# Four moves in the written order of steps of a fused mLSTM cell and GELU layer

## The chip, the cores and the metric

The kernel runs on one core of a Trainium2 chip. The metric is device time in microseconds (us). Engines work side by side, each through its own queue in the order in which the program gives instructions: PE (matrix multiplies), DVE (vector), ACT (activation functions), POOL (GpSimd) and SP, which here issues most DMA transfers. An engine whose next instruction waits does nothing else in the meantime.

## The reference, cut to what matters

First an mLSTM cell over `q, k, v, o_gate` of shape (4, 8, 768, 40) and gates `i_gate, f_gate` of shape (4, 8, 768), then a two-layer feed-forward block with exact GELU:

```python
for t in range(S):
    m_new = maximum(f[t] + m, i[t])
    f_stab, i_stab = exp(f[t] + m - m_new), exp(i[t] - m_new);  m = m_new
    C = f_stab * C + i_stab * outer(v[t], k[t])
    n = f_stab * n + i_stab * k[t]
    y[t] = sigmoid(o[t]) * (C @ q[t]) / maximum(abs(n @ q[t]), 1)
x = y.transpose(0, 2, 1, 3).reshape(3072, 320)
out = gelu_exact(x @ w_in) @ w_out        # w_in 320 x 2048, w_out 2048 x 320
```

## The kernel before

The sequence of 768 is cut into six chunks of 128, numbered 0 to 5. Within a chunk the recurrence is written as attention with decays, and only a state of each head goes from chunk to chunk. The four batch entries of a chunk are called turns 0 to 3 here; each has eight heads. Each chunk's 512 rows of y then go through the feed-forward block. From chunk 1 on, its matrix products are made of three products of split operands (a high part, a low part and a sum, named `hi`, `lo` and `mid` or `all`).

The work of two chunks is interleaved: while the feed-forward block of chunk c runs, the cell of chunk c+1 is computed, and the cell of chunk c+2 is begun. Nothing schedules this but strings written by hand. Each word of a string is a step, a letter with an index, and `play` calls the steps from left to right; an engine's queue is what falls to it in that order. `FRONT` holds chunk 0 and all preparation, `SECOND` the feed-forward block of chunk 1 with the cell of chunk 2, `LATER` those of chunks 2, 3 and 4, and `LAST` that of chunk 5. An index of 4 or more on a cell letter means the cell after next: `M4` is turn 0 of it.

The steps that the change touches, or that stand next to it:

- `U0` to `U3` (`up`, L1055 and L1061 on PE): the four parts of x @ w_in into PSUM tiles `pu`, two at a time from the same banks as other steps of the cell.
- `g0` to `g15` (`gelu`): block n of 128 hidden features. ACT does GELU (L1068, `g_whole`) and the high part (L1069), then DVE the low part (L1070) and the rest (L1071). The first GELU after other functions has an ACT table load in front of it.
- `d0` to `d15` (`down`, L1075 on PE): block n times `w_out`, three products for each of four turns.
- `y0` to `y15` (`out_mid`, L1030 on DVE): the sum part of the weights for `d` of that index, in one of four places `w_out_mid`, which are used in turn.
- `i5` to `i14` (`load_in`, L1004 on SP): the reload of a stored sum part of `w_in` (256 KB each) into one of five places. `i10` and `i11` bring the parts that the next chunk's `U0` reads.
- `M` (`mask`, L469 on POOL) and `W` (`weights`, L495 on ACT): the masking and the exponentials of a turn's decay matrix, tile `W`, which `B` (`load_M`, L211 on SP) brings as two 512 KB loads.
- `K` and `Q` in `LATER`, `(` and `)` in `FRONT` (`turn_k`, `turn_q`, L511 on DVE): the transposing of a turn's k and q from `blocks` into `kT` and `qT`. `L` and `[` (`load_blocks`, L189 on SP) load `blocks` from the copies `kq_d`, which `+` (L180 on SP) makes in DRAM.
- `C`, `h` (PE L620, L631): the state read and its update. `D` (L538 on POOL): values times decays, tile `vw`.
- `S` (`scores_two`) multiplies scores into `W` (L573 on DVE); `V` (`values`, PE L657 and DVE L662).
- `Y` (`finish`, L671 to L674 and L679 on DVE): five steps for a turn's gated and normalised y, in tile `ob`.
- `t` (`twice`, L686, on ACT from chunk 2 on): a small copy of a turn's last 64 columns of y, twice, into `y_rest`.
- `X` (`turn_y`, PE L695, ACT L705): the transposing of a turn's y from `ob` and `y_rest` into `px`, and the high part of x. `R` (`split_x`, DVE L716 and L717): its other parts.
- `J` and `O` (`load`, L171 and L173 on SP): k, v and gate loads. `F` in `FRONT` (L959 on PE): chunk 0 times `w_out`, one row block at a time; `a` and `b` (ACT L1015, DVE L1022) prepare parts of `w_out`.

The word `t0` means `twice(0)`: it needs the result of `Y0`, and `X0` needs it. `y_rest` is one tile for all turns, so `t1` also waits until PE has read what `t0` wrote.

Of the kernel before, what the change touches and what calls it, by code (L numbers as in the profile page):

```python
# [28 lines left out]
    g1 c1 J y1 s2 K x0 t3 x1 v2 g2 O4 J B4 g3 c2 y2 s3 B5 K x2 K L5 J T0 K v3 A y3 M1 x3 c3 G0 M0 H O7 O6 O5 J  # L29
    J i5 u0 L6 u1 K W0 J W1 I4 A K S0 T1 C0 J j5 i6 V0 i7 u2 G2 K U M2 L7 S1 J G1 K U i8 j6 W2 J j7 i9 C1 T2 K  # L30
    M3 f2 S2 V1 Y0 T3 J Y1 C2 e j8 W3 j9 K K K J S3 J C3 f3 K X0 B8 J K R0 B9 h5 J h6 h7 K J V2 K Y2 J J Z Z K
    K V3 X1 J K r F J h8 h9 F a0 a1 F K b0 b1 F a2 a3 F b2 b3 F F F J K X2 G3 F F J K J Y3 F J K R1 a4 a5 b4 b5 a6 b6 K B10 p + + + + F X3 a7 b7 F J J Z Z R2 R3
    a8 F (0 )0 [1 Z a9 a10 <0 <1 >0 >1 a11 a12 a13 a14 a15 z0 z1 b8 b9 b10 b11 b12 b13 b14 b15 B11 F F """
CELL = "MWGVYXRKQDCSht"
LATER = """
    U0 E0 E1 E2 E3 K1 Q1 L2 D0 D1 y0 y1 y2 y3 C0 h0 M2 M3 g0 g1 g2 g3 i5 i6 +
    U1 i7 i8 i9 g4 d0 g5 y4 d1 g6 y5 d2 g7 y6 S0 d3 K2 Q2 L3 y7 W2 W3 G0 G1 G2 G3 +
    U2 i10 i11 g8 d4 g9 V0 V1 K3 Q3 B4 B5 J0 J1 d5 g10 d6 g11 S2 L4 d7 y8 y9 y10 y11
    U3 + M4 M5 Y0 Y1 D2 D3 K4 W4 W5 t0 i12 i13 i14 g12 d8 g13 y12 d9 g14 X0 t1 R0 y13 d10 g15 X1 R1 C2 h2 O0 O1 d11 V2 Y2 t2 y14 B6 J2 d12 V3 Y3 Q4 L5 y15 B7 d13 X2 t3 R2 d14 X3 R3 d15 + O2 O3"""

SECOND = """
    z2 U0 z3 z4 K1 Q1 L2 D0 D1 y0 y1 y2 y3 C0 h0 M2 M3 g0 g1 g2 g3 i5 i6 + +
    U1 i7 i8 i9 g4 d0 g5 y4 d1 g6 y5 d2 g7 y6 S0 d3 K2 Q2 L3 y7 W2 W3 G0 G1 G2 G3 +
    U2 i10 i11 + g8 d4 g9 V0 V1 K3 Q3 B4 B5 J0 J1 d5 g10 d6 g11 S2 L4 d7 y8 y9 y10 y11
    U3 + M4 M5 Y0 Y1 D2 D3 K4 W4 W5 t0 i12 i13 i14 g12 d8 g13 y12 d9 g14 X0 t1 R0 y13 d10 g15 X1 R1 C2 h2 O0 O1 d11 V2 Y2 t2 y14 B6 J2 d12 V3 Y3 Q4 L5 y15 B7 d13 X2 t3 R2 d14 X3 R3 d15 + O2 O3"""

LAST = """
    U0 E0 E1 E2 E3 y0 y1 y2 y3 g0 g1 g2 g3 U1 i5 i6 i7 i8 i9 x y12 y13 y14 y15 g4 d0 g5 y4 d1 g6 y5 d2 g7 y6 d3 y7
# [1141 lines left out]
```

## Time and profile before

| what | value |
|---|---|
| time, median of 3 runs | 452.74 us (451.29 to 452.99) |
| the profiled execution, time | 450.36 us |
| its span, first to last instruction | 448.6 us |
| PE busy | 435.4 us (97%) |
| DVE busy | 352.7 us (79%) |
| ACT busy | 283.9 us (63%) |
| POOL busy | 54.3 us (12%) |
| granted TensorE clock | 0.999 |
| U0 of chunks 1 to 5 starts at | 121.2, 192.0, 259.4, 327.1, 391.1 us |

All times of instructions below are counted from the start of the span. In a timeline row stand start, duration, engine, line, operation, tiles written and read, shapes and count, and in brackets the idle time of the engine ahead of it with what released it. In a row of the page's groups stand busy time and mean duration, and behind the bar the idle time ahead of the group's instructions and its releaser. `SPq` is SP's queue issuing DMA transfers.

### The profile page before, as it was taken

The numbers are of one execution on the slowest core, as the hardware profiler recorded it, in microseconds if no ns is written. First come the engines' busy times: TensorE is split into PE (matmuls) and PEld (weight loads), VectorE is DVE, ScalarE is ACT, GpSimd is POOL, SyncE is SP. The second block draws the span as 40 slices with busy tenths as digits, with TensorE's granted clock in tenths as the row PEclk, the third lists the DMA queues.
The fourth block names the chain that finished last, engine by engine and source line by source line (L and its number), as shares of the span: only waits on it lengthen the run. The fifth ranks groups of instructions, "written<-read, shape, count | busy, mean of one in ns | idle before, by whom it ended". The sixth has DMA issues, their size and how long they took to land.

```text
span 448.6 us, 13147 instructions
## 1 busy us (share of the span) xinstructions
PE 435.4 (97%) x5320; PEld 375.5 (84%) x5320; DVE 352.7 (79%) x759; ACT 283.9 (63%) x603; POOL 54.3 (12%) x82
## 2 busy tenths in 40 slices
PE   8999999999999998999999999999999999999996
PEld 7778788777778897888898888898888898989986
DVE  8797788877989599959599959599969598847540
ACT  4989999858958939137968037958137925244441
POOL 3001123030030022221021211021110000000000
PEclk9999999999999999999999999999999999999999
DMA  7998995898297478466687365696466412032001
GB/s 154 212 212 219 206 237 150 208 286 216 95 241 189 101 205 165 92 135 144 138 217 148 90 135 136 143 212 124 94 143 170 79 31 72 1 108 70 1 1 58
DMA packets 165785, 63.24 MB, mean 141 GB/s; under 512 B 148413, under 2 KB 151773, under 8 KB 165469
## 3 DMA queue, kind: packets, MB, share of 16 engines
q1 hardware_dynamic: 165004, 60.76, 58.2%
q0 software_dynamic: 400, 1.31, 0.7%
q8 instruction: 42, 0.69, 0.7%
q10 hardware_dynamic: 320, 0.33, 0.2%
q14 instruction: 19, 0.15, 0.1%
HBM read 55.63 MB, written 11.99 MB: 151 GB/s over the span
## 4 chain that ended last, share of the span: by engine, by line
PE 62%; DVE 12%; issue 10%; DMA 8%; ACT 5%; POOL 2%; SPq 1%; POOLq 0%; DVEq 0%; ACTq 0%
PE po L1075 21%; PE pu L1055 20%; PE pu L1061 6%; DMA W<-M_d 5%; PE po L959 4%; DMA kq_d<-in_q_dram 3%; PE pu L789 2%; ACT W L495 2%; DVE w_out_mid L1030 2%; DVE g_parts L1071 2%; PE ps L567 2%; PE ph L657 2%; DVE g_parts L1070 1%; PE pf L620 1%; PE px L695 1%
## 5 line engine op out<-in xcount | busy, mean ns | idle before, releaser
L1070 DVE SCALAR_TENSOR_TENSOR g_parts<-g_whole,g_parts 128x512 fp32r<-128x512 f32 x80 | 56.7, 709 | 43.4 <-ACT g_parts L1069 43.1
L1068 ACT ACTIVATE g_whole<-pu 128x512 f32<-128x512 f32 x80 | 47.4, 593 | 60.3 <-PE pu L1061 40.2
L1075 PE MATMUL po<-w_out_mid,g_parts 128*128 128x320 f32 x320 | 58.5, 299 | 0.0
L1069 ACT ACTIVATE g_parts<-g_whole 128x512 fp32r<-128x512 f32 x80 | 50.5, 631 | 8.8 <-PE po L1075 6.6
L1071 DVE TENSOR_TENSOR g_parts<-g_whole,g_parts 128x512 fp32r<-128x512 f32 x80 | 55.3, 691 | 0.0
L1055 PE MATMUL pu<-x_hi,w_in_hi 128*128 128x512 f32 x160 | 48.4, 384 | 0.2 <-DVE W L573 0.2
L1075 PE MATMUL po<-w_out_hi,g_parts 128*128 128x320 f32 x240 | 48.5, 316 | 0.0
L1075 PEld LDWEIGHTS po<-w_out_mid,g_parts 128*128 128x128 f32 x320 | 48.4, 189 | 0.0
L1055 PE MATMUL pu<-x_all,w_in_mid 128*128 128x512 f32 x160 | 47.6, 379 | 0.0
L1075 PE MATMUL po<-w_out_lo,g_parts 128*128 128x320 f32 x240 | 44.6, 299 | 0.0
L469 POOL TENSOR_SCALAR_AFFINE_SELECT W<-W 128x1024 f32<-128x1024 f32 (+2 forms) x20 | 22.2, 1111 | 153.2 <-DMA W<-M_d 144.6
L1075 PEld LDWEIGHTS po<-w_out_hi,g_parts 128*128 128x128 f32 x240 | 35.6, 190 | 4.4 <-issue 3.3
L495 ACT ACTIVATE W<-W,aT 128x128 f32<-128x128 f32 x128 | 38.8, 388 | 0.4 <-POOL W L469 0.3
L1075 PEld LDWEIGHTS po<-w_out_lo,g_parts 128*128 128x128 f32 x240 | 36.5, 189 | 0.2 <-issue 0.2
L959 PE MATMUL po<-w_out,g 128*128 128x320 f32 x128 | 35.0, 432 | 0.0
L1030 DVE TENSOR_TENSOR w_out_mid<-w_out_hi,w_out_lo 128x320 fp32r<-128x320 f32 x60 | 34.0, 588 | 0.1
L1055 PEld LDWEIGHTS pu<-x_all,w_in_mid 128*128 128x128 f32 x160 | 30.2, 189 | 4.3
L1055 PEld LDWEIGHTS pu<-x_hi,w_in_hi 128*128 128x128 f32 x160 | 29.1, 189 | 4.3 <-PE po L1075 0.4
L686 ACT COPY y_rest<-ob 128x128 f32<-128x128 f32 x16 | 4.7, 294 | 43.9 <-DVE ob L679 43.9
L959 PEld LDWEIGHTS po<-w_out,g 128*128 128x128 f32 x128 | 24.1, 190 | 9.7
L1075 PE MATMUL po<-w_out_part,g_parts 128*128 128x320 f32 x160 | 25.9, 305 | 0.0
L1075 PEld LDWEIGHTS po<-w_out_part,g_parts 128*128 128x128 f32 x160 | 22.5, 189 | 1.9 <-issue 1.7
(195 smaller groups left out, 835.9 us busy)
## 6 DMA issues: line engine op xcount, KB each, us to landing
w_in_mid<-w_in_mid_d SPq DMA_DIRECT2D x36, 256.0 KB, 6.6
W<-M_d SPq DMA_DIRECT2D x16, 512.0 KB, 6.6
bits<-in_moe_w_in_dram SPq DMA_DIRECT2D x20, 256.0 KB, 4.4
bits<-in_moe_w_out_dram SPq DMA_DIRECT2D x16, 320.0 KB, 4.9
blocks<-kq_d SPq DMA_DIRECT2D x32, 128.0 KB, 3.3
ob<-in_o_gate_dram SPq DMA_DIRECT2D x24, 160.0 KB, 5.9
out_dram<-o_sb SPq DMA_DIRECT2D x36, 80.0 KB, 2.0
g_parts<-w_in_mid_d SPq DMA_DIRECT2D x9, 256.0 KB, 5.8
```

What stands on the lines that cost most here:

```text
L469: nc.gpsimd.affine_select(out=x, in_=x, compare_op=OP.is_ge, fill=1.0e30, base=base, pattern=[[0, H], [1, x.shape[2]]], channel_multiplier=-1)
L495: nc.scalar.activation(out=W[n][:, h, :], in_=src, func=AF.Exp, scale=-1.0, bias=aT[:, self.c, r:r + 1])
L567: nc.tensor.matmul(ps[i][hip][halves[x ^ i], p, t], kT[i][r, p, halves[x]], qT[i][r, p, t], start=True, stop=True)
L959: nc.tensor.matmul(po[b], g.t[:, f, b * L:(b + 1) * L], w_row(n), start=(n == 0), stop=(n == NF - 1))
L1030: nc.vector.tensor_tensor(out=to, in0=hi, in1=lo, op=OP.add)
L1055: nc.tensor.matmul(in_pairs(pus[i][e]), w3(at[k])[n][:, e, i * P:(i + 1) * P], in_turns(x3[n][:, k, :]), start=(n == 0 and k == 0), stop=F ...
L1061: nc.tensor.matmul(in_pairs(pus[i][e]), w3(r)[n][h, q % 2, i * P:(i + 1) * P], in_turns(x3[n][h, NX, :]), start=False, stop=(n == 2), skip ...
L1068: nc.scalar.activation(out=whole, in_=self.pus[n // 4][n % 4 // 2][n % 2], func=AF.Gelu, scale=4097.0)
L1069: nc.scalar.activation(out=hi, in_=whole, func=AF.Copy, scale=PART)
L1070: nc.vector.scalar_tensor_tensor(out=lo, in0=whole, scalar=-1.0 / BASE, in1=hi, op0=OP.mult, op1=OP.add)
L1071: nc.vector.tensor_tensor(out=rest, in0=whole, in1=hi, op=OP.subtract)
L1075: nc.tensor.matmul(in_pairs(self.po[t]), x[:, t * L:(t + 1) * L], in_turns(w), start=(n == 0 and k == 0), stop=(n == NF - 1 and k == 2), s ...
```

## The change

No instruction is added or removed; four kinds of step move in the strings.

1. `(0 )0`, which transpose turn 0 of the third chunk's cell (chunk 2), move in `FRONT` from behind `a8 F` to ahead of the first `F`, behind `h9`. On DVE they come ahead of the first L1022 and of everything that stood between.
2. `y8 y9 y10 y11` stood at the end of the `U2` row. Now `Y0` comes first, then `y8 y9`, `Y1`, `y10 y11`.
3. `t0` stood ahead of `i12 i13 i14 g12`; now it stands behind `g12`.
4. `i10 i11` stood directly behind `U2`; now they stand directly ahead of `i12`. On SP they are passed by a copy into `kq_d` (`SECOND` alone), the two loads of `W`, the loads of k and v, a load of `blocks` and another copy into `kq_d`.

Moves 2 to 4 are in `SECOND` and in `LATER`, so they happen in chunks 1, 2, 3 and 4.

```diff
 FRONT = """
...
-    K V3 X1 J K r F J h8 h9 F a0 a1 F K b0 b1 F a2 a3 F b2 b3 F F F J K X2 G3 F F J K J Y3 F J K R1 a4 a5 b4 b5 a6 b6 K B10 p + + + + F X3 a7 b7 F J J Z Z R2 R3
-    a8 F (0 )0 [1 Z a9 a10 <0 <1 >0 >1 a11 a12 a13 a14 a15 z0 z1 b8 b9 b10 b11 b12 b13 b14 b15 B11 F F """
+    K V3 X1 J K r F J h8 h9 (0 )0 F a0 a1 F K b0 b1 F a2 a3 F b2 b3 F F F J K X2 G3 F F J K J Y3 F J K R1 a4 a5 b4 b5 a6 b6 K B10 p + + + + F X3 a7 b7 F J J Z Z R2 R3
+    a8 F [1 Z a9 a10 <0 <1 >0 >1 a11 a12 a13 a14 a15 z0 z1 b8 b9 b10 b11 b12 b13 b14 b15 B11 F F """
...
 LATER = """
...
-    U2 i10 i11 g8 d4 g9 V0 V1 K3 Q3 B4 B5 J0 J1 d5 g10 d6 g11 S2 L4 d7 y8 y9 y10 y11
-    U3 + M4 M5 Y0 Y1 D2 D3 K4 W4 W5 t0 i12 i13 i14 g12 d8 g13 y12 d9 g14 X0 t1 R0 y13 d10 g15 X1 R1 C2 h2 O0 O1 d11 V2 Y2 t2 y14 B6 J2 d12 V3 Y3 Q4 L5 y15 B7 d13 X2 t3 R2 d14 X3 R3 d15 + O2 O3"""
+    U2 g8 d4 g9 V0 V1 K3 Q3 B4 B5 J0 J1 d5 g10 d6 g11 S2 L4 d7
+    U3 + M4 M5 Y0 y8 y9 Y1 y10 y11 D2 D3 K4 W4 W5 i10 i11 i12 i13 i14 g12 t0 d8 g13 y12 d9 g14 X0 t1 R0 y13 d10 g15 X1 R1 C2 h2 O0 O1 d11 V2 Y2 t2 y14 B6 J2 d12 V3 Y3 Q4 L5 y15 B7 d13 X2 t3 R2 d14 X3 R3 d15 + O2 O3"""
...
 SECOND = """
...
-    U2 i10 i11 + g8 d4 g9 V0 V1 K3 Q3 B4 B5 J0 J1 d5 g10 d6 g11 S2 L4 d7 y8 y9 y10 y11
-    U3 + M4 M5 Y0 Y1 D2 D3 K4 W4 W5 t0 i12 i13 i14 g12 d8 g13 y12 d9 g14 X0 t1 R0 y13 d10 g15 X1 R1 C2 h2 O0 O1 d11 V2 Y2 t2 y14 B6 J2 d12 V3 Y3 Q4 L5 y15 B7 d13 X2 t3 R2 d14 X3 R3 d15 + O2 O3"""
+    U2 + g8 d4 g9 V0 V1 K3 Q3 B4 B5 J0 J1 d5 g10 d6 g11 S2 L4 d7
+    U3 + M4 M5 Y0 y8 y9 Y1 y10 y11 D2 D3 K4 W4 W5 i10 i11 i12 i13 i14 g12 t0 d8 g13 y12 d9 g14 X0 t1 R0 y13 d10 g15 X1 R1 C2 h2 O0 O1 d11 V2 Y2 t2 y14 B6 J2 d12 V3 Y3 Q4 L5 y15 B7 d13 X2 t3 R2 d14 X3 R3 d15 + O2 O3"""
```

## The prediction

> **What bounds the kernel now.** I read the page first, then PE's waits and timeline, then the timeline of all engines around each wait. By the page PE is busy nearly throughout, so only a stop of PE can be won back. The copy y_rest, which the change moves, sits behind 43.9 us of ACT idle time.
>
> ```profile
> PE 435.4 (97%) x5320; PEld 375.5 (84%) x5320; DVE 352.7 (79%) x759; ACT 283.9 (63%) x603; POOL 54.3 (12%) x82
> ...
> L686 ACT COPY y_rest<-ob 128x128 f32<-128x128 f32 x16 | 4.7, 294 | 43.9 <-DVE ob L679 43.9
> ```
>
> ACT is busy 63% of the span, so those 43.9 us are not a sum to claim. From 131 us on, PE's timeline shows real stops almost only at the transposes px (L695) near the end of a chunk, between the fourth up step (U3) and the next U0. Brackets give idle time and releaser.
>
> ```profile
> 177.85 0.33 PE L695 MATMUL px<-ident,y_rest 128*128 128x128 f32 x1 [1.45 <-ACT y_rest L686]
> ...
> 187.51 0.41 PE L695 MATMUL px<-ident,ob 128*128 128x128 f32 x2 [0.32 <-DVE ob L679]
> ...
> 254.91 0.41 PE L695 MATMUL px<-ident,ob 128*128 128x128 f32 x2 [0.31 <-DVE ob L679]
> ...
> 312.93 0.33 PE L695 MATMUL px<-ident,y_rest 128*128 128x128 f32 x1 [0.64 <-ACT y_rest L686]
> ...
> 324.96 0.41 PE L695 MATMUL px<-ident,ob 128*128 128x128 f32 x2 [0.72 <-DVE ob L679]
> ...
> 386.67 0.71 PE L1075 MATMUL po<-w_out_mid,g_parts 128*128 128x320 f32 x4
> 387.21 0.38 PE L695 MATMUL px<-ident,ob 128*128 128x128 f32 x2
> ```
>
> The last two rows, chunk 4, are undisturbed: px starts 0.54 after the group before it, and y_rest 0.22 after ob. Against those spacings chunk 1 loses 0.35+1.62+0.49+0.35 = 2.8 us, chunk 2 0.25+0.48+0.35 = 1.1, chunk 3 0.80+0.88 = 1.7, chunk 4 nothing: 5.6 us, the ceiling for the U3 edits. What leads to these stops, in chunk 2:
>
> ```profile
> 222.13 0.85 SPq L1004 DMA_DIRECT2D w_in_mid<-w_in_mid_d  x2
> ...
> 225.21 0.96 SPq L211 DMA_DIRECT2D W<-M_d  x2
> ...
> 231.73 1.28 ACT L495 ACT_TABLE_LOAD   x1 [2.83 <-DMA W<-M_d]
> ...
> 233.48 1.95 POOL L469 TENSOR_SCALAR_AFFINE_SELECT W<-W 64x1024 f32<-64x1024 f32 x2 [0.59 <-DMA W<-M_d]
> ...
> 234.27 3.38 DVE L1030 TENSOR_TENSOR w_out_mid<-w_out_hi,w_out_lo 128x320 fp32r<-128x320 f32 x4
> 235.51 1.79 POOL L538 TENSOR_TENSOR vw<-vb,ewT 128x328 f32<-128x328 f32 x2
> ...
> 238.61 0.49 DVE L679 TENSOR_TENSOR ob<-ob,den 128x320 f32<-128x320 f32 x1
> ...
> 239.14 0.30 ACT L686 COPY y_rest<-ob 128x128 f32<-128x128 f32 x1 [1.23 <-DVE ob L679]
> ...
> 239.46 1.28 ACT L1068 ACT_TABLE_LOAD   x1
> ...
> 240.47 0.70 DVE L511 STREAM_TRANSPOSE kT<-blocks 128x512 f32<-128x512 f32 x1
> ...
> 242.04 0.69 DVE L1070 SCALAR_TENSOR_TENSOR g_parts<-g_whole,g_parts 128x512 fp32r<-128x512 f32 x1 [0.87 <-ACT g_parts L1069]
> ```
>
> The loads W release the masks and exps; DVE does four sums, then Y0, which frees ACT's copy, gelu and split; DVE waits 0.87 for that split. From 242.04 to the last ob at 257.14 DVE has no idle row: an earlier L1070 passes on one for one to the px that stop PE. Chunks 1 and 3 read the same.
>
> **The front's two turns.** (0 and )0 are two L511 of 0.70 and 0.67 us. They leave 119.20 on DVE for a place after 101.2, where DVE idles 1.70 us for ACT before the L1022 at 102.87; their blocks were asked for at 76.08 and such a load lands in 4.2 us, so they do not wait. If that cover were gone they would cost 1.3 us of DVE, not of PE. The freed 1.3 us at 119 brings w_in_lo and the first w_in_mid earlier for U0, whose first pair at 121.17 shows 0.24 more than its spacing: at most 0.24. PE's 1.01 stop at 129.87 stays: it waits for the next turn, whose block loads SP issued at 121.84 and 124.78 because of the copies into kq_d, which do not move. Taken as 0.
>
> **Gelu ahead of the copy (t0).** The copy's 1.23 us wait (chunks 2 and 3; none in chunk 1) and its 0.30 leave the path to block 12. The exps end at 171.85, 237.91, 305.59; table 1.28, gelu 0.60, split 0.63 and gaps make ACT ready for L1070 at 174.4, 240.5, 308.2, instead of 174.64, 242.04, 309.72. Next late is DVE itself, whose kT turn ends at 173.81, 241.17, 309.21. The copy now delays block 13 by 0.30; DVE needs 1.2 us a block, so that hides. X0 reads y_rest later still (242.8 in chunk 2). In chunk 4 the gelu waits 1.18 us for PE's own products: nothing to win.
>
> **Y0 ahead of the sums.** PE's and POOL's orders do not change; on DVE the same instructions come in another order: Y0, two sums, Y1, two sums. The sums write w_out_mid places whose readers (d4 to d7) end before U3; d8 reads y8's first at 240.64, d10 y10's at 244.23: two us of slack or more. But POOL's masks and products run beside this stretch, and DVE pays:
>
> ```profile
> 368.31 1.70 DVE L1030 TENSOR_TENSOR w_out_mid<-w_out_hi,w_out_lo 128x320 fp32r<-128x320 f32 x4
> ...
> 169.45 0.70 DVE L672 TENSOR_SCALAR den<-far 128x8 f32<-128x8 f32 x1
> ```
>
> Four sums take 1.70 without POOL (chunk 4), 3.38 beside it; Y0's small L672 takes 0.70 beside it, 0.16 without. So each step, large or small, gets about one POOL instruction (0.8 to 1.2 us). Filling those slots with Y0's five short steps instead of sums of 0.43 does less work in them: in chunk 2 POOL's ends (234.56, 235.43, 236.36, 237.30) put Y0's end at 237.8, and 0.85+1.53+0.85+0.71 more ends kT at 241.74, 0.57 later than now. Alone this leaves L1070 earlier by 0.3 in chunks 2 and 3 (309.44 there) and 0.2 in chunk 1: 0.8 us in all. Without the port effect the sum would be 0.2+0.87+0.51 = 1.6. The Trainium skill, SBUF — State Buffer, Summary: rules for kernel authors, has a DVE operation with two SBUF inputs block fully until a GpSimd operation that reads SBUF ends. The sums agree with it, and it speaks against this edit. By its letter L672 and L674, with one input, would pass: kT in chunk 2 at about 241.3, and 1.4 us in all; the 0.70 row says otherwise.
>
> **Reloads i10, i11 moved on.** On SP they pass the W loads (B4, B5), the k and v loads, the blocks load (L4) and copies into kq_d, and now stand ahead of i12. Their issue takes 0.85 us; SP waits for PE's ph before W anyway, so issue wins nothing. Their 0.5 MB does: issued 3.1 us before W, on the same SP queue. DMA moved 171 GB/s in 223 to 226 and 285 GB/s in 226 to 229, other copies among it. If all had been gone by 225.21, W lands no sooner (0); if none, 0.52 MB / 285 GB/s = 1.8 us sooner. By 225.21 perhaps half had moved: I take 0.9. Both masks and exps follow W, so ACT is ready 0.9 sooner and POOL's slots begin beside L573, which they do not lengthen (1.78 against 1.76 in chunk 4). Redone with 0.9: kT ends near 173.9, 241.1, 308.8 (blocks, 0.27 late in chunk 3, come earlier too), so L1070 gains about 0.8, 0.9, 0.9. The reloads' own reader, U0, comes 17 us or more after the new place; a load takes 6.6. What they now share DMA with, gate loads and copies, is read a stage later; if that cover went, U0 would stand for the lateness.
>
> **Sum.** 0 + 0.8 + 0.9 + 0.9 + 0 = 2.6 us, within each chunk's stops. The profiled execution took 450.36 (span 448.6 and 1.8 around it), 0.5% below the median 452.74 of three runs (451.29 to 452.99): 447.8 on its scale, 450.1 on the median's. A measurement can tell 0.5%, 2.26 us, from no change.
>
> **Rivals.** *Small gain*: W lands no sooner and Y0 fills POOL's slots: 0.8 us, 451.9. For it: 3 us of head start for the reloads; against it: the 285 GB/s right after, DMA saturated. *All stops go*: W comes 1.8 sooner and PE bounds the tails: 4 to 5.5 us, about 448. For it: W took 9.3 us to land in chunk 1 against 6.4 in chunk 2. Against: DVE stays contiguous. *Slower*: POOL's slots stretch over Y0 and also y8 and y9, two more blocked steps of 0.85 each in chunks 1 to 3. It decides once kT ends over 0.5 to 0.9 us later than now (L1070's present idle). Taking 0.57 for Y0 and 1.7 more, less slack of 0.82, 0.87, 0.51, costs 1.4+1.4+1.8 = 4.6 us: 457.3. Against: POOL has only four or five instructions there. *The turns do nothing*: part of every case.
>
> **Numbers.** Forecast 0.50 (gain 1.9 to 3.4, four fifths of it over 2.26), small gain 0.26, all stops 0.12, slower 0.12. Faster by over 0.5%: 0.40+0.12 = 0.52; slower 0.12; the rest 0.36. The range runs from 447.8 (most of the large case) to 453.4 (small gain plus the runs' spread of 0.7 and more), leaving out the slower case.
>
> **What would show it.** Right: y_rest's first copy of each chunk without idle time and after block 12's split; L1070 of block 12 within 0.2 us of kT's end in chunks 1 to 3; exps starting 0.5 to 1.5 us sooner after the W issue; px stops of 5.6 us down to about 3; the 129.87 stop unchanged. Wrong: W's landing unchanged, Y0 over 3.5 us, a new PE stop at d8, U0 or the state products.

## The result and the profile after

The changed kernel took **446.52 us** (median of six runs, 445.73 to 450.05); the kernel before took 452.83 beside it (six runs, 451.29 to 454.54). The ratio is 0.9879, with a 95% interval of 0.9838 to 0.992: by the ratio 5.5 us less. The kernel was measured twice more in the experiments below, at ratios of 0.9916 and 0.9898 (3.8 and 4.6 us less). The three together put the gain near **4.6 us**, against a forecast of 2.6, and the first median lies 1.3 us below the forecast's range. Two executions, the profiled ones of the repeat of after and of the copy alone below, ran at a lower granted clock (0.852 and 0.657) and are left out of every median, ratio and profile reading.

The profiled execution of after took 449.06 us (span 447.3, granted clock 1.0), only 1.3 us less than the one of before (450.36). That pair understates the gain. U0 of chunk 1 starts at 122.32 in it against 121.17, and over all profiled executions that start lies between 120.6 and 122.8 whichever edits the kernel has. So the executions are compared below by the stretch from U3 to the next U0, the tail of a chunk:

| profiled execution | chunk 1 | chunk 2 | chunk 3 | sum, us |
|---|---|---|---|---|
| before, first profile | 28.46 | 26.69 | 27.24 | 82.4 |
| before, a second profile | 29.27 | 26.82 | 26.95 | 83.0 |
| after, first profile | 28.03 | 26.04 | 25.46 | 79.5 |
| after, a second profile | 26.50 | 26.04 | 25.13 | 77.7 |

The tail of chunk 4 is 24.38 in every one of them. The means of the pairs differ by 4.1 us: most of what was gained was gained here.

The page of after, in the engines' row and the groups (busy time and mean, and behind the bar idle time before and its releaser):

```profile
PE 435.6 (97%) x5320; PEld 376.0 (84%) x5320; DVE 350.3 (78%) x759; ACT 283.9 (63%) x603; POOL 54.6 (12%) x82
...
L1030 DVE TENSOR_TENSOR w_out_mid<-w_out_hi,w_out_lo 128x320 fp32r<-128x320 f32 x60 | 29.1, 502 | 0.0
...
L686 ACT COPY y_rest<-ob 128x128 f32<-128x128 f32 x16 | 4.7, 291 | 32.1 <-DVE ob L679 32.1
```

PE does the same work. The idle time ahead of y_rest fell from 43.9 to 32.1: the first copy of each chunk no longer waits, the later ones do. The sums L1030 fell from 34.0 to 29.1 us of busy time, because fewer of them now run beside POOL.

PE's timeline of after, the rows at the four turns' transposes (bracket: idle time before, and its releaser):

```profile
131.31 0.68 PE L620 MATMUL pf<-state,qT 64*64 64x41 f32 x32 [1.31 <-DVE qT L511]
...
178.52 0.33 PE L695 MATMUL px<-ident,y_rest 128*128 128x128 f32 x1 [1.06 <-ACT y_rest L686]
...
188.39 0.38 PE L695 MATMUL px<-ident,ob 128*128 128x128 f32 x2 [0.53 <-DVE ob L679]
...
257.54 0.41 PE L695 MATMUL px<-ident,ob 128*128 128x128 f32 x2 [0.18 <-DVE ob L679]
...
312.59 0.27 PE L695 MATMUL px<-ident,y_rest 128*128 128x128 f32 x1
...
323.57 0.41 PE L695 MATMUL px<-ident,ob 128*128 128x128 f32 x2
```

Chunk 1 keeps stops, chunk 2 a trace, and chunk 3 (last two rows) has none with a bracket any more. The stop near 130 stays, as forecast. What leads to chunk 3's transposes, in the timeline of all engines, with U3 starting at 300.20:

```profile
292.86 0.98 SPq L211 DMA_DIRECT2D W<-M_d  x2
...
297.51 1.28 ACT L495 ACT_TABLE_LOAD   x1 [0.96 <-DMA W<-M_d]
...
303.13 0.16 DVE L672 TENSOR_SCALAR den<-far 128x8 f32<-128x8 f32 x1
...
306.50 0.60 ACT L1068 ACTIVATE g_whole<-pu 128x512 f32<-128x512 f32 x1 [1.37 <-PE pu L1061]
...
307.23 0.70 DVE L511 STREAM_TRANSPOSE kT<-blocks 128x512 f32<-128x512 f32 x1
...
307.67 0.28 ACT L686 COPY y_rest<-ob 128x128 f32<-128x128 f32 x1
...
307.86 0.65 DVE L1070 SCALAR_TENSOR_TENSOR g_parts<-g_whole,g_parts 128x512 fp32r<-128x512 f32 x1
```

W releases ACT 4.65 us after its issue; the kernel before needed 6.84 there. Gelu stands ahead of the copy and now waits 1.37 us for PE's own products: ACT is no longer late. L1070 follows kT at once, 7.66 us after U3 instead of 9.90. L672 takes 0.16, so POOL's slots no longer reach it. In chunk 2 (U3 at 233.59) they do:

```profile
226.24 1.19 SPq L211 DMA_DIRECT2D W<-M_d  x2
...
230.72 1.28 ACT L495 ACT_TABLE_LOAD   x1 [0.80 <-DMA W<-M_d]
...
230.80 1.44 POOL L469 TENSOR_SCALAR_AFFINE_SELECT W<-W 128x1024 f32<-128x1024 f32 x1 [26.50 <-DVE g_parts L1071]
...
231.21 1.57 DVE L1071 TENSOR_TENSOR g_parts<-g_whole,g_parts 128x512 fp32r<-128x512 f32 x1
...
234.37 1.80 POOL L469 TENSOR_SCALAR_AFFINE_SELECT W<-W 64x1024 f32<-64x1024 f32 x2 [2.13 <-DMA W<-M_d]
...
236.44 0.70 DVE L672 TENSOR_SCALAR den<-far 128x8 f32<-128x8 f32 x1
...
237.17 0.66 DVE L673 SCALAR_TENSOR_TENSOR den<-far,den 128x8 f32<-128x8 f32 x1
...
238.50 0.89 DVE L1030 TENSOR_TENSOR w_out_mid<-w_out_hi,w_out_lo 128x320 fp32r<-128x320 f32 x2
...
241.56 0.70 DVE L511 STREAM_TRANSPOSE kT<-blocks 128x512 f32<-128x512 f32 x1
...
242.19 0.65 DVE L1070 SCALAR_TENSOR_TENSOR g_parts<-g_whole,g_parts 128x512 fp32r<-128x512 f32 x1
```

The first load of W came after 4.48 us (before: 6.52), but POOL waited 2.13 us for the second, whose mask starts 8.13 us after the issue (before: 8.27). The masks end at the old time, Y0's small steps stand in POOL's slots (0.70 and 0.66), and L1070 gains 0.75.

The sooner W also costs something in this chunk. Its first mask now runs beside the L1071 of block 11, which takes 1.57 us. In the kernel before, where that mask came later, it took less than half:

```profile
230.17 0.69 DVE L1071 TENSOR_TENSOR g_parts<-g_whole,g_parts 128x512 fp32r<-128x512 f32 x1
```

DVE therefore starts on Y0 and the sums 2.2 us after U3 instead of 1.6. Over all the profiles used of kernels that have these masks, in chunks 2 and 3, this L1071 takes 1.57 or 1.58 wherever W releases ACT within 4.75 us of its issue (six cases, all with the reloads moved), and 0.68 or 0.69 wherever it takes 4.89 or longer. In the kernel below that leaves these masks out it takes 0.69 although ACT goes on 3.71 us after the issue.

### The profile page after: what moved, and what is told of

Its sections match the earlier page's. It is cut to its first block, busy times and chain, and to the rows that moved or that the text cites. A ratio compares the mean times of both kernels' runs of the same rounds, so it can differ in the third digit from the quotient of the medians.

```text
span 447.3 us, 13126 instructions
## 1 busy us (share of the span) xinstructions
PE 435.6 (97%) x5320; PEld 376.0 (84%) x5320; DVE 350.3 (78%) x759; ACT 283.9 (63%) x603; POOL 54.6 (12%) x82
## 3 DMA queue, kind: packets, MB, share of 16 engines
q0 software_dynamic: 400, 1.31, 0.7%
## 4 chain that ended last, share of the span: by engine, by line
PE 74%; DVE 10%; DMA 8%; ACT 4%; SPq 2%; issue 2%; DVEq 0%; ACTq 0%
PE po L1075 25%; PE pu L1055 21%; PE pu L1061 6%; PE po L959 4%; PE ph L657 3%; DMA kq_d<-in_q_dram 3%; PE pu L789 2%; PE ps L567 2%; DMA bits<-in_moe_w_in_dram 2%; PE pu L818 2%; DMA blocks<-kq_d 2%; DVE g_parts L1071 2%; PE pf L620 1%; DVE g_parts L1070 1%; PE px L695 1%
## 5 line engine op out<-in xcount | busy, mean ns | idle before, releaser
L1070 DVE SCALAR_TENSOR_TENSOR g_parts<-g_whole,g_parts 128x512 fp32r<-128x512 f32 x80 | 56.3, 703 | 41.6 <-ACT g_parts L1069 41.2
L1071 DVE TENSOR_TENSOR g_parts<-g_whole,g_parts 128x512 fp32r<-128x512 f32 x80 | 57.7, 722 | 0.0
L1075 PE MATMUL po<-w_out_lo,g_parts 128*128 128x320 f32 x240 | 44.4, 299 | 0.0
L1030 DVE TENSOR_TENSOR w_out_mid<-w_out_hi,w_out_lo 128x320 fp32r<-128x320 f32 x60 | 29.1, 502 | 0.0
L686 ACT COPY y_rest<-ob 128x128 f32<-128x128 f32 x16 | 4.7, 291 | 32.1 <-DVE ob L679 32.1
```

What stands on the lines that cost most here:

```text
L1030: nc.vector.tensor_tensor(out=to, in0=hi, in1=lo, op=OP.add)
L1070: nc.vector.scalar_tensor_tensor(out=lo, in0=whole, scalar=-1.0 / BASE, in1=hi, op0=OP.mult, op1=OP.add)
L1071: nc.vector.tensor_tensor(out=rest, in0=whole, in1=hi, op=OP.subtract)
L1075: nc.tensor.matmul(in_pairs(self.po[t]), x[:, t * L:(t + 1) * L], in_turns(w), start=(n == 0 and k == 0), stop=(n == NF - 1 and k == 2), s ...
```

## Experiments

The theory is the prediction's: the tails are held by DVE's chain up to L1070, and the gain comes out of it by an earlier W, an earlier Y0 and a gelu that doesn't wait for Y0. The rivals: the moves of steps on DVE and ACT do everything and the reloads nothing, or the reverse; the front's two turns bring something; POOL's slots cost more than the forecast has. Twelve further measurements were made, each in five rounds beside the kernel before on the same chip.

| kernel | median, us | ratio to before | 95% interval | tails, sum, us |
|---|---|---|---|---|
| after, repeat | 447.18 | 0.9916 | 0.9885 to 0.9948 | |
| after, third | 447.96 | 0.9898 | 0.9866 to 0.993 | 77.7 |
| before, repeat | 452.40 | 1.0003 | 0.9976 to 1.003 | 83.0 |
| reloads alone | 450.29 | 0.9968 | 0.9946 to 0.9989 | 81.4 |
| copy alone | 449.76 | 0.9961 | 0.9939 to 0.9982 | |
| front alone | 451.79 | 0.9998 | 0.9973 to 1.0023 | 82.6 |
| Y0 alone | 448.92 | 0.9923 | 0.99 to 0.9947 | 80.6 |
| after without Y0's move | 447.09 | 0.9892 | 0.9866 to 0.9919 | 77.7 |
| after without the copy's | 447.52 | 0.992 | 0.9887 to 0.9953 | 77.8 |
| after without the reloads' | 449.87 | 0.9958 | 0.9927 to 0.999 | 81.5 |
| before, two masks left out | 449.72 | 0.997 | 0.9947 to 0.9992 | 80.8 |
| after, W ahead of `kq_d` | 450.21 | 0.9965 | 0.9937 to 0.9993 | 80.1 |

### The two kernels again

No edit.

> The changed kernel as it is, for a second profile of it. The first pair of profiles differs by 1.3 us, the medians by 6.3. Tails below are the stretches from U3's start to the next U0's start in chunks 1, 2 and 3: 28.46+26.69+27.24 = 82.39 us before, 28.03+26.04+25.46 = 79.53 in the first profile after, so 2.86 less; up to U0 of chunk 1 that profile was 1.14 later. Theory A (tails alone): the tails again sum to 79 to 80, U0 of chunk 1 varies by 1 to 2 us between executions of either kernel, and five rounds give 2.5 to 3.5 us under the kernel before. Theory B (the front's turns): up to U1 of chunk 1 this execution is 2 to 3 us shorter than the kernel before, and the time is 5 to 6 us under it. Theory C (tails win more than that pair showed): tails at 79 or less here and at 84 to 86 in most executions of the kernel before, time 5 to 6 us under.

> The kernel before as it is, for a second profile of it; its time against itself is the same within 1 us. Theory A: tails 81.5 to 83, U0 of chunk 1 anywhere from 121 to 124. Theory B: U0 or U1 of chunk 1 at 123 to 125, two or three us later than the changed kernel's. Theory C: tails 84 to 86, with loads W landing later than 9.3, 6.4 and 6.8 us after their issue.

> The changed kernel again, for a second undisturbed profile beside the runs of this call: 4 to 5 us under the kernel before. Theory A: tails of chunks 1 to 3 sum to 79 to 80 us against 82.4 and 83.0 in the two profiles of the kernel before. Theory B: tails as that, and the stretch from 86.3 to U1 of chunk 1 below 44.4.

Measured: 3.8 and 4.6 us less for after, nothing for before against itself. The gain is real and above the forecast in each of the three measurements, but the first, at 5.5, is the largest of them.

### The reloads alone

```diff
-    U2 i10 i11 g8 d4 g9
+    U2 g8 d4 g9
...
-    K4 W4 W5 t0 i12 i13 i14 g12
+    K4 W4 W5 t0 i10 i11 i12 i13 i14 g12
```

> The kernel before with i10 and i11 moved on, nothing else. Theory A: W lands about 0.9 us sooner in chunks 1 to 3, POOL's masks and the exps follow, but the copy still waits for Y0 behind four sums; the tails lose 0.3 to 0.5 each, 1 to 1.5 us in all. Theory C: W's landing is what most of the gain hangs on: tails shorter by 2.5 or more, 3 to 5 us in time. Theory B: nothing, within 0.5 us.

Measured: 1.4 us less. W lands sooner, but in chunks 1 and 2 that is not used: their tails are 28.85 and 26.76, as before, and all that the tails show (25.81 against 27.24 and 26.95) is in chunk 3. Chunk 3 in the timeline of this kernel:

```profile
294.50 0.98 SPq L211 DMA_DIRECT2D W<-M_d  x2
...
299.82 1.28 ACT L495 ACT_TABLE_LOAD   x1 [1.62 <-DMA W<-M_d]
...
307.82 0.30 ACT L686 COPY y_rest<-ob 128x128 f32<-128x128 f32 x1 [1.63 <-DVE ob L679]
...
310.72 0.69 DVE L1070 SCALAR_TENSOR_TENSOR g_parts<-g_whole,g_parts 128x512 fp32r<-128x512 f32 x1 [0.86 <-ACT g_parts L1069]
```

W releases ACT 5.32 us after its issue; five profiled executions of kernels whose reloads did not move have 6.7 to 7.4 here. ACT then stands 1.63 us at the copy, which waits for Y0 behind the sums, and L1070 still waits 0.86 for ACT. An earlier W needs one of the two moves behind it to be used in full.

### The copy alone

```diff
-    W4 W5 t0 i12 i13 i14 g12 d8
+    W4 W5 i12 i13 i14 g12 t0 d8
```

> The kernel before with t0 behind g12, nothing else. Theory A: ACT no longer waits for Y0's result in chunks 2 and 3; L1070 of block 12 comes 0.2, 0.9 and 0.5 us sooner in chunks 1, 2, 3: 1.6 us in tails and time. Theory B: the same 1.6 in the tails, and 4 us still missing to the changed kernel. Theory C: under 1 us, since late W loads and not the copy hold ACT.

Measured: 1.75 us less, as theory A has it. No profile at the full clock was taken, so in which chunks the gain lies is not shown.

### Y0 alone

```diff
-    S2 L4 d7 y8 y9 y10 y11
-    U3 + M4 M5 Y0 Y1 D2 D3
+    S2 L4 d7
+    U3 + M4 M5 Y0 y8 y9 Y1 y10 y11 D2 D3
```

> The kernel before with Y0 and Y1 put ahead of pairs of the sums, nothing else: t0 still stands ahead of g12, but its source is done four sums sooner. The prediction's port term: Y0's five short steps beside POOL's instructions each last about one of these, Y0 ends 0.3 us later than the four sums did, kT 0.3 to 0.6 later; against that the copy waits less. By it 0.2 to 0.8 us faster. Rival D (short steps slip between POOL's instructions at 0.16 to 0.20, as they did in chunk 1 of the changed kernel's first profile): kT no later than before, the copy done before the exps end, 1.3 to 1.8 us faster.

Measured: 3.5 us less by the ratio, far more than the order was worth in the forecast. (The profiled execution of this kernel, 450.93, was the slowest of its runs, and its tails show 1.8 to 2.5 of it.) In it Y0 ends 5.19, 4.02 and 4.19 us after U3 instead of 8.08, 6.42 and 6.96, so the copy, still ahead of gelu, starts without idle time in all three chunks: moving Y0 cures the same wait as moving the copy. The cost that the forecast set against it did not appear. Chunk 2, U3 at 234.61:

```profile
236.85 0.62 DVE L672 TENSOR_SCALAR den<-far 128x8 f32<-128x8 f32 x1
...
237.51 0.17 DVE L673 SCALAR_TENSOR_TENSOR den<-far,den 128x8 f32<-128x8 f32 x1
...
238.55 1.43 DVE L1030 TENSOR_TENSOR w_out_mid<-w_out_hi,w_out_lo 128x320 fp32r<-128x320 f32 x2
...
242.14 0.70 DVE L511 STREAM_TRANSPOSE kT<-blocks 128x512 f32<-128x512 f32 x1
```

Only some of Y0's steps are lengthened: L672 takes 0.62, but L673 passes at 0.17, and the two sums behind Y0 take what is left of POOL's time (1.43, against 0.89 in the changed kernel). Y0 does not need one POOL instruction for each step. In chunks 1, 2 and 3 kT ends 9.95, 8.23 and 9.30 us after U3; in the three profiles without any move between U2 and U0 it ends 10.28 to 10.51, 8.44 to 8.96 and 8.71 to 9.39. The order itself costs kT nothing that these profiles can tell.

### After without the move of Y0, and without that of the copy

```diff
-    S2 L4 d7
-    U3 + M4 M5 Y0 y8 y9 Y1 y10 y11 D2 D3
+    S2 L4 d7 y8 y9 y10 y11
+    U3 + M4 M5 Y0 Y1 D2 D3
```

> The changed kernel with the four sums put back ahead of Y0 and Y1. If the order is worth nothing or costs, as the prediction's port term has it, this is as fast as the changed kernel or up to 0.6 us faster: 4 to 5 us under the kernel before. By rival D the sums again stand ahead of Y0 and lengthen by POOL's instructions: 1 us or more slower than the changed kernel.

```diff
-    i10 i11 i12 i13 i14 g12 t0 d8
+    t0 i10 i11 i12 i13 i14 g12 d8
```

> The changed kernel with t0 put back ahead of i10 and g12. Theory A, refined: the copy and the order cure the same wait. In the changed kernel Y0 ends 4.1 to 5.0 us after U3's start, ahead of or with the last exps, so the copy finds its source done and costs ACT its 0.3 alone: within 0.6 us of the changed kernel, 4 to 5 us under the kernel before. Rival E (the single gains of 1.75, 3.5 and 1.45 are of different waits and would add): 1.5 us or more slower than the changed kernel.

Measured: 447.09 and 447.52, with tails of 77.7 and 77.8. Neither can be told from after. Chunk 2 of the kernel without Y0's move, U3 at 231.18:

```profile
223.84 0.97 SPq L211 DMA_DIRECT2D W<-M_d  x2
...
228.19 1.28 ACT L495 ACT_TABLE_LOAD   x1 [0.66 <-DMA W<-M_d]
...
233.44 2.44 DVE L1030 TENSOR_TENSOR w_out_mid<-w_out_hi,w_out_lo 128x320 fp32r<-128x320 f32 x4
...
238.65 0.28 ACT L686 COPY y_rest<-ob 128x128 f32<-128x128 f32 x1
238.69 0.70 DVE L511 STREAM_TRANSPOSE kT<-blocks 128x512 f32<-128x512 f32 x1
...
239.32 0.65 DVE L1070 SCALAR_TENSOR_TENSOR g_parts<-g_whole,g_parts 128x512 fp32r<-128x512 f32 x1
```

Y0 stands behind the sums again, yet kT ends 8.21 us after U3, sooner than in the two profiles of after (8.67, 8.49). The sums take POOL's slots (2.44 for four), Y0's small steps run free, and with the copy behind gelu nobody on ACT waits for Y0. That kT is sooner is no price of Y0's order: with Y0 first and the copy's move taken back, kT ends 8.20 after U3 in chunk 2. So the two moves are two cures of one wait: beside the moved reloads either does the work of both. The single gains (0, 1.75, 3.5 and 1.4, together 6.7) fit that by adding to more than the 4.6 of the whole, but this difference alone is no larger than the intervals leave open.

### After without the move of the reloads

```diff
-    U2 g8 d4 g9
+    U2 i10 i11 g8 d4 g9
...
-    W4 W5 i10 i11 i12 i13 i14 g12 t0
+    W4 W5 i12 i13 i14 g12 t0
```

> The changed kernel with i10 and i11 put back behind U2. Theory A: W lands 9.2, 6.2 and 6.8 us after its issue in chunks 1, 2, 3 again, against 7.4 to 8.5, 4.4 and 4.6 to 5.2 in the changed kernel, POOL's masks run beside Y0 and the sums again, L1070 of block 12 starts 0.5 to 1.5 us later in chunks 1 and 3; 1 to 2 us slower than the changed kernel, 2.5 to 3.5 under the kernel before. If W's landing does not matter any more once ACT is free of the copy: within 0.5 us of the changed kernel.

Measured: 1.9 us less than before, where after without the copy's move, measured beside it, has 3.6 and the three measurements of after 4.6 in the mean: about half of the gain is gone. Between those two neighbours the intervals overlap (0.9927 to 0.999, 0.9887 to 0.9953); their tails, 81.5 and 77.8, say the same more clearly. Chunk 3 of this kernel (all engines, then PE):

```profile
293.18 0.96 SPq L211 DMA_DIRECT2D W<-M_d  x2
...
300.61 1.28 ACT L495 ACT_TABLE_LOAD   x1 [3.74 <-DMA W<-M_d]
...
309.72 0.68 DVE L1070 SCALAR_TENSOR_TENSOR g_parts<-g_whole,g_parts 128x512 fp32r<-128x512 f32 x1
...
325.31 0.41 PE L695 MATMUL px<-ident,ob 128*128 128x128 f32 x2 [1.08 <-DVE ob L679]
```

W needs 7.43 us, L1070 is back at 9.33 after U3, and PE has its stop again. This is the move that the others do not replace. Taken over ten profiled executions, all but those of the two kernels below that leave out masks or put W ahead of the copies, five with the reloads at their old place and five with them moved, the times from W's issue are (means in us, chunks 1, 2, 3):

| from the issue of W | reloads unmoved | moved | sooner by |
|---|---|---|---|
| to ACT's table load (first load landed) | 9.30, 6.09, 6.96 | 8.11, 4.72, 4.91 | 1.2, 1.4, 2.0 |
| to the second load's mask on POOL | 10.80, 8.07, 8.84 | 9.58, 7.77, 7.09 | 1.2, 0.3, 1.8 |
| to the end of the exps | 15.53, 12.51, 13.28 | 14.26, 12.08, 11.38 | 1.3, 0.4, 1.9 |

The 0.3 and 0.4 of chunk 2 lie within what executions differ by (the second mask 7.79 to 8.27 unmoved and 7.31 to 8.13 moved); the other differences are larger than that or nearly so.

### The front's two turns alone

```diff
-    J h8 h9 F a0 a1 F
+    J h8 h9 (0 )0 F a0 a1 F
...
-    a8 F (0 )0 [1 Z
+    a8 F [1 Z
```

> The kernel before with (0 and )0 moved to ahead of the first F, nothing else. Theory A (tails alone): within 0.5 us of the kernel before; the stretch from chunk 0's first product with w_out (86.3 in the first profile) to U1 of chunk 1 (131.2) stays at 44.9 within 0.5, and the stop at the state read of chunk 2 stays, since the next block loads wait for the copies into kq_d. Theory B (the turns matter): 1 to 2.5 us faster, that stretch shorter by as much, and the sum of the single moves closes on the whole 4 us.

Measured: nothing, as forecast; the stretch from chunk 0's first product with w_out to U1 of chunk 1 is 44.0 us, against 44.9 and 44.4 in the two profiles of before. DVE in after, around the new place and the next turn's kT:

```profile
102.12 0.70 DVE L511 STREAM_TRANSPOSE kT<-blocks 128x512 f32<-128x512 f32 x1
...
103.91 0.89 DVE L1022 SCALAR_TENSOR_TENSOR w_out_part<-w_out_part,w_out 128x320 fp32r<-128x320 f32 x2 [0.49 <-ACT w_out_part L1015]
...
129.95 0.71 DVE L511 STREAM_TRANSPOSE kT<-blocks 128x512 f32<-128x512 f32 x1 [1.74 <-DMA blocks<-kq_d]
```

The turns fill DVE's idle time (1.70 became 0.49), and the time set free later becomes a longer wait of DVE for `blocks` (1.01 became 1.74).

### Before, with two masks left out

In the kernel before, the masks of turns 0 and 1 of the cell after next (M4, M5) are left out of SECOND and LATER, so that their decays are not masked. Nothing else is changed.

```diff
-    U3 + M4 M5 Y0 Y1 D2 D3
+    U3 + Y0 Y1 D2 D3
```

> The kernel before without M4 and M5 in chunks 1, 2 and 3 (the masks of turns 0 and 1 of the cell after next are left out), so that POOL has only its two products beside the four sums. It measures the port term by itself. If POOL's instructions hold DVE up as the prediction has it: the four sums take 1.7 to 2.5 us instead of 3.4 to 3.9, Y0 and with it the copy, the gelu and L1070 come 1 to 2 us sooner in each of chunks 1 to 3, tails sum to 78 to 80 us. If DVE's lengthened rows are only an effect of how spans are drawn: tails stay at 82 to 83.

Measured: 1.4 us less by the ratio. DVE in chunk 2, U3 at 233.65:

```profile
235.31 1.70 DVE L1030 TENSOR_TENSOR w_out_mid<-w_out_hi,w_out_lo 128x320 fp32r<-128x320 f32 x4
...
241.98 0.71 DVE L511 STREAM_TRANSPOSE kT<-blocks 128x512 f32<-128x512 f32 x1 [1.52 <-DMA blocks<-kq_d]
```

Without the masks beside them the four sums take 1.70 instead of 3.38, and Y0 ends 5.35 us after U3 instead of 6.42 (3.3 sooner in chunk 1, 1.6 in chunk 3). That POOL's masks lengthen DVE's steps is shown. What their absence would give is then mostly taken by the next wait: kT stands 1.52 for its `blocks`, and the tails sum to 80.8, above the 78 to 80 expected and below the 82 to 83 of the other reading.

### After, with W ahead of the copies into kq_d

SECOND alone, so chunk 1 alone: the two loads of W pass the two copies that `+` makes.

```diff
-    W2 W3 G0 G1 G2 G3 +
-    U2 + g8 d4 g9 V0 V1 K3 Q3 B4 B5 J0 J1
+    W2 W3 G0 G1 G2 G3
+    U2 g8 d4 g9 V0 V1 K3 Q3 B4 B5 + + J0 J1
```

> The changed kernel with the two copies into kq_d around U2 of chunk 1 moved behind the two W loads. If what still holds chunk 1 is W landing 7.4 to 8.5 us after its issue, behind those copies: W lands 4.5 to 6 us after its issue there as in chunks 2 and 3, chunk 1's tail falls from 26.5 to 28 us to 25.3 to 26.3, and the time is 0.5 to 1.5 us under the changed kernel. Rival: the blocks for kT, loaded from these copies, come later and DVE waits for them instead; chunk 1's tail as it is or longer.

Measured: 450.21, or 1.6 us less than before by the ratio, where after without the copy's move, measured beside it, has 3.6. Chunk 1 (all engines, then PE), U3 at 163.90:

```profile
160.49 1.28 ACT L495 ACT_TABLE_LOAD   x1 [0.43 <-DMA W<-M_d]
...
174.73 0.71 DVE L511 STREAM_TRANSPOSE kT<-blocks 128x512 f32<-128x512 f32 x1 [3.44 <-DMA blocks<-kq_d]
...
178.53 0.33 PE L695 MATMUL px<-ident,y_rest 128*128 128x128 f32 x1 [2.08 <-ACT y_rest L686]
```

W lands 4.08 us after its issue (8.45 and 7.38 in the two profiles of after), the exps end 3.0 to 4.1 us sooner after U3, and all of it is lost: kT stands 3.44 us for `blocks` and ends 11.54 after U3 instead of 10.45 and 8.97. The rival of the expectation is what happened: the copies that W passed come later, and with them the `blocks` that are loaded from them. It also shows why W needs longer in chunk 1 than in the others: there the copies into `kq_d` are ahead of it.

## Why the prediction was right or wrong

**What was right in the mechanism.** The time went out of the tails of chunks 1 to 3, through L1070 of block 12, and about one for one: against the three profiles without the U3 moves (before, its repeat, the front alone) L1070 starts 1.55, 0.84 and 2.04 us sooner after U3 in the two profiles of after, 4.4 us in all, and their tails are 1.5, 0.65 and 1.9 shorter, beside some 4.6 timed. Forecast were 0.8, 0.9 and 0.9. Two terms of that sum failed, and chunk 2 came out right only because their errors cancelled there.

**The first step that failed is the price set on Y0's order.** The forecast had 1.6 us for the copy and Y0 together, and took it down to 0.8 because each of Y0's steps, large or small, was to last about one POOL instruction. The runs show no such cost. In the two kernels that have Y0's order with the reloads at their old place (Y0 alone, after without the reloads' move) L1070 starts 0.3, 1.1 and 0.55 us sooner than in the kernel before, 1.9 in all, close to the forecast's own 0.2, 0.87 and 0.51 that leave this cost out. In the mean kT ends 0.1 and 0.3 us sooner in chunks 1 and 2 and 0.3 later in chunk 3, within what executions differ by; the forecast had it 0.57 later in chunk 2. By their times these two kernels gain 3.5 and 1.9. That the masks lengthen what runs beside them is right (four sums 1.70 without them). But their time falls on whichever steps stand there, and then on the sums behind; it is not paid once for each step.

**The second is the 0.9 us for W's sooner landing.** It was taken as the middle between 0 and 1.8, with half of the reloads' bytes assumed gone by the time of W's issue, and the same in all chunks. Measured at the exps it is 1.3, 0.4 and 1.9. At L1070 the forecast gave it 0.6 a chunk on top of the other moves. The four profiles with the reloads and at least one of the other two moves lie 1.3, 0.0 and 1.5 below the two without the reloads' move, 2.7 in all instead of 1.8. In chunk 2 only the first load comes clearly sooner, and in three of those four profiles its mask then costs DVE 0.9 us at L1071, ahead of L573; the forecast had POOL's slots begin beside L573, where they cost nothing. In chunk 3 POOL was nearly or wholly done when Y0 came (L672 0.16 in the first profile of after, 0.70 in the second), and kT ends 7.73 and 7.99 us after U3, where the forecast's 308.8 means 8.98.

**Ceiling and chances.** The px stops counted against chunk 4's spacings gave 5.6 us. The shortest tails that any run shows in chunks 2 and 3 are 25.1 us, 1.6 and 2.1 below the first profile's, where the stops counted were 1.1 and 1.7: the ceiling was set some 0.4 a chunk too low. *All stops go* was given 0.12, against "DVE stays contiguous". DVE did stay contiguous, but L1070's earlier start was passed on whole. In chunk 3 that rival is what the second profile of after shows, with 25.13 us; chunk 2, with 26.04, and chunk 1 kept a part of their stops.

**Two cures priced as a pair.** That the move of Y0 and that of the copy would each do alone the work of both was not seen. For the whole that changed nothing.

The prediction's reading of the Trainium skill was incomplete. SBUF — State Buffer, Summary: rules for kernel authors, of the Trainium skill names DVE operations in a 2-port performance mode beside those with two SBUF inputs, and its section Who interferes with whom counts `tensor_scalar` among those that can enter such a mode. So by the Trainium skill L672 may be held up as well, and its 0.70 agrees with that; which mode it ran in, no run here shows.

**Right:** no gain from the front's turns; the stop near 130 still there (1.01, 1.31; over the executions used it varies from none to 1.98, and not by the place of the turns); no new stop at d8, U0 or the state products; the first y_rest copy of each chunk without idle time and behind block 12's split; L1070 at kT's end in all three chunks. The *slower* rival (POOL's slots over y8 and y9 too) occurred in no tail: the two sums behind Y0 take 0.89 in chunks 2 and 3 of after, and in chunk 1, where they do take 1.88, kT still ends no later than 10.45 after U3, against 10.28 to 10.51 without the moves. *Small gain* fell because W did land sooner.

**Open.** Why U0 of chunk 1 starts up to 2.2 us apart in executions of kernels that hardly differ before it, and what in the traffic sets how much sooner the second load of W lands, was not tried. Why Y0 alone timed 3.5 us while its tails show 1.8 to 2.5, and both moves without the reloads 1.9, is within what the intervals allow and was not settled.

## What to carry to other kernels

A load that is moved out of the way of an urgent one is worth pricing chunk by chunk, with both halves of the urgent load, and with both ends of the bound kept: here one edit gave 0.4 us in one chunk and 1.9 in the next. Moves that cure the same wait do not add: with the reloads moved, taking back either Y0's move or the copy's lost nothing that could be told. One that looks small alone can be the one that the others lack: the reloads brought L1070 forward by 0.9 us in all alone and by 2.7 in company. Before a load is pulled ahead, ask which load it passes, who waits for that one next, and beside which steps its own reader will now run.

## What the runs showed that was not expected

Of two 512 KB loads issued within about 1 us, the removal of 0.5 MB ahead of them moved the first by 1.4 us in chunk 2 and the second by 0.3 at most, which is within the spread, but both by 1.8 to 2.0 in chunk 3. Landing sooner was not always good: where the first load came within 4.75 us, POOL's mask met L1071 of block 11, which then took 1.57 us instead of 0.69. Passing two copies instead took 3.3 to 4.4 us off the landing of W in chunk 1, and kT, which waits for a load behind them, ended 1.1 to 2.6 us later after U3.
